# Scores two steps ahead, side products in front of the exponential, and both products of split factors in the tail

## The chip, the cores and the metric

The kernel runs on one core of a Trainium2 chip. A core has engines that run side by side, each its own row of instructions in order: TensorE (PE) for matrix products and transposes, VectorE (DVE), ScalarE (ACT) and GpSimd (POOL) for work on tiles, SyncE (SP) for issuing transfers. They wait for each other by semaphores. Tiles lie in SBUF, results of TensorE in PSUM. The metric is the time of one execution in microseconds of the device. Before the change it is 1297.87 us, the median of three runs (1297.45 to 1298.43).

## The reference

8 batches of 8 heads, 576 positions of 64 numbers: the scores of each row keep only their 32 largest, a softmax follows, and the product with the values is a row of x (4608 rows of 512). Then a mixture of 8 experts: each row goes to the expert with the largest logit.

```python
scores = scale * np.matmul(q, k.transpose(0, 1, 3, 2))
kth = np.partition(scores, -top_k, axis=-1)[..., -top_k:-top_k + 1]
scores = np.where(scores >= kth, scores, -1000000000.0)
attn = softmax(scores)            # exp(s - max) / (sum + 1e-09)
x = matmul(attn, v)               # to [N, 512]
logits = x @ w_gate
e_idx = np.argmax(logits, axis=1)
for e in range(E):
    mask = e_idx == e
    h = np.maximum(x[mask] @ w1[e], 0.0)      # 512 -> 1024
    ye = h @ w2[e]                            # 1024 -> 512
    out[mask] = gate_w[mask, None] * eom[mask, e, None] * ye
```

## The kernel before

The rows of x are 36 tiles of 128, each with 8 heads in 4 pairs: 144 steps i of one tile and one head pair. The order of instructions on every engine is that of the code of the main loop; there is no scheduler behind it, only small queues of work (urgent, small, later) from which a step takes some, with a budget per step (SUMS for scaling x on GpSimd, DMAS for gathering lists).

One step handles several head pairs at different stages. On VectorE: rank(i), which finds the eight by eight largest of 64 candidates; window(i-1), the maxima over a masked copy w; the maxima of groups of 72 scores for step i+1 (line 302); choose(i-1), which picks the 32nd largest (line 362, on 8 columns); weigh(i-1), which masks the exponentials with it (line 378). On ScalarE: the copy of scores(i+1) out of PSUM (line 283), the marks of step i by a Sign function (line 336), the exponentials (line 346), and copies of transposed weights. On GpSimd: w = scores + marks (line 339). On TensorE: scores(i+1) (line 275), flip(i-2), which transposes the weights in parts of 4, 1 and 4 chunks (line 404; copies to pT at line 412), and attend, the product with the values for two head pairs in every second step (line 436).

In the first 48 steps (LONE), which run ahead of the slots of the experts, VectorE masks only one of the two heads. The other is masked by ScalarE and GpSimd: veil (a Sign, line 385, and an addition, line 388) and in the next step unveil, an exponential with its sum (line 394). These steps also do 12 idle transposes on TensorE (line 895).

After the fourth pair of a tile come side products: in one step the gates (line 466: four products for the logits, and two transposes of xT), in the next the rows (line 475 transposes lt, the logits; line 457 two chunks of xT). They write the same PSUM tile as chunk 4 of a flip, pst, of which there are two buffers; their copies are lt (line 470) and xu (line 460). x is scaled by GpSimd (line 479) in two halves of 0.6 us each by the planner's cost; with SUMS = 1.3 both fit into one step.

Rows are sorted by expert in groups of tiles. A slot is 128 rows of one expert with its weights w1 and w2 (2 MB each, two buffers each). There are 40 slots; 25 run in pieces inside steps 51 to 143, in fp32 (line 714 up, line 729 down), and 15 after the last step, in the tail (slots_in_turn). In the tail before, the up products are fp32, and the down products use split factors: w2 and h are each parted into a high and a low part of type fp32r (lines 997, 998, 1005, 1006), and three products high x high, high x low, low x high replace one (line 1015). The table of the last group's slots is worked out by 26 small VectorE operations (lines 598 to 639) at the start of the tail.

Of the kernel before, what the change touches and what calls it, by code (L numbers as in the profile page):

```python
# [10 lines left out]
F32 = mybir.dt.float32  # L11
# [12 lines left out]
P = 128  # L24
# [5 lines left out]
USUAL = 11  # L30


SUMS = 1.3
DMAS = 2.0

NLIST = 12
# [3 lines left out]
def tile_topk_attention_moe(  # L40
# [89 lines left out]
    def setup():  # L130

        def iota(x, pattern, base=0, mult=0):
            return lambda: nc.gpsimd.iota(x, pattern=pattern, base=base, channel_multiplier=mult,
                                          allow_small_or_imprecise_dtypes=True)

        def gates():
            for a in range(2):
                for i, w in enumerate((w_gate, w_out_gate)):
                    c0 = a * 16 + i * 8
                    nc.sync.dma_start(  # L140
                        wg[a * 64:(a + 1) * 64, :, c0:c0 + E],
                        w.rearrange("(c a p) e -> a p c e", a=2, p=64)[a])

        at = entry.rearrange("p (b j) o -> p b j o", j=9)
        S2, NBP = 2 * S, NB // 2
        ops = [lambda: nc.gpsimd.memset(wg, 0.0), gates,
               lambda: nc.gpsimd.memset(ones, 1.0), lambda: nc.gpsimd.memset(ones_b, 1.0),
               iota(before, [[1, P]], 0, -1),
               lambda: nc.gpsimd.tensor_scalar(before, before, 0.0, None, op0=ALU.is_gt),
               lambda: nc.vector.tensor_copy(before_b, before),  # L150
               iota(first, [[-1, E]], E), iota(carry0, [[REG, E]]),
               lambda: nc.gpsimd.memset(first_row, 0.0),
               iota(slot_iota, [[1, MAXS], [0, E]], 1), iota(slot_off, [[P, MAXS]]),
               iota(entry[:, :, 0], [[P, NTT]], 0, 1),
               iota(at[:, :, 0:4, 1], [[S2, NBP], [P, 4]], 0, 1),
               iota(at[:, :, 5:9, 1], [[S2, NBP], [P, 4]], S, 1),
               iota(at[:64, :, 4, 1], [[S2, NBP]], 4 * P, 1),
               iota(at[64:, :, 4, 1], [[S2, NBP]], S + 4 * P, 1),
               lambda: nc.gpsimd.memset(entry[:, :, 3], 0)]
        ops += [lambda m=m: nc.gpsimd.memset(m, 0.0) for m in pads.values()]  # L160
        return ops
# [23 lines left out]
    def run(exact, stack):  # L185
# [141 lines left out]
        def below(i):  # L327
            vs = VV[i][0]
            ep = wk.tile([P, 2, S], F32, name="ep", bufs=3)
            EP[i] = ep  # L330
            if not exact:
                n = wk.tile([P, 2], F32, name="n", bufs=3)
                SW[i] = ([], n)
                for a in range(2):
                    s, m = SC[i, a], marks[a]
                    nc.scalar.activation(m.bitcast(I8).rearrange("p (s b) -> p s b", b=2)[:, :, 1], s, AF.Sign,  # L336
                                         bias=vs[:, a, PIVOT - 1:PIVOT], scale=-(1.0 + 2.0 ** -20), accum_out=n[:, a:a + 1])
                    w = wk.tile([P, S], F32, name="w", bufs=3)
                    nc.gpsimd.tensor_tensor(w, s, m, op=ALU.add)  # L339
                    SW[i][0].append(w)  # L340
# [56 lines left out]
        def flip(i, part, extra=None):  # L397
# [4 lines left out]
            ps = ps_t.tile([P, 4, P], F32, name="pst")  # L402
            for c in range(c0, c1):
                nc.tensor.transpose(ps[:, c - c0, :], pt[:, c * P:(c + 1) * P], ident)  # L404
            ev = extra(ps) if extra else None
# [467 lines left out]
        for i in range(NSTEP + 4):  # L873
            t, hp = divmod(i, NHP)
            step[0] = i
            if i + 1 < NSTEP:
                scores(i + 1)()
            for r in range(3):
                if i < NSTEP:
# [100 lines left out]

        def slots_in_turn():

            def prepare(n):
                ahead("id", fetch_id, n + 2)
                ahead("x", fetch_x, n + 1)
                ahead("w1", fetch_w1, n)
                ahead("w2", fetch_w2, n)

            def turned(n):
                ahead("turn", lambda s, *_: turn(s, pools["p"], "pm")(), min(n, had["x"] - cur[0]))  # L990

            def split(s, part):

                w = W[s][1][:, 4 * part:4 * part + 4]
                hi, lo = [pools["w"].tile([P, 4, DM], F32R, name=n, bufs=3) for n in ("w2h", "w2l")]
                HL[s, part] = hi, lo
                nc.scalar.activation(hi, w, AF.Copy)
                nc.vector.tensor_tensor(lo, w, hi.bitcast(F32), op=ALU.subtract)

            def up_split(s, f0):  # L1000
                if f0 == 0:
                    HT[s] = [pools["w"].tile([P, NF, P], F32R, name=n, bufs=1) for n in ("hth", "htl")]
# [5 lines left out]
            def down_split(s, f0):  # L1008
                if f0 == 0:
                    PY[s] = pools["p"].tile([P, DM], F32, name="pm")  # L1010
                hh, hl = HT[s]
                wh, wl = HL.pop((s, f0 // 4))
                for f in range(f0, f0 + 4):
                    for k, (h, w) in enumerate(((hh, wh), (hh, wl), (hl, wh))):
                        nc.tensor.matmul(PY[s], h[:, f, :], w[:, f - f0, :], start=(f == 0 and k == 0),
                                         stop=(f == NF - 1 and k == 2))

            def splitted(s, part):
                if s < min(len(order), had["w2"]) and (s, part) not in HL:
                    split(s, part)  # L1020
            while cur[0] < len(order):
                s = cur[0]
                prepare(1)
                turned(1)
                prepare(2)
                splitted(s, 0)
                splitted(s, 1)
                ahead("w2", fetch_w2, 3)
                for f0 in (0, 4):
                    up_split(s, f0)  # L1030
# [96 lines left out]
```

## Time and profile before

| | |
|---|---|
| median of the runs | 1297.87 us |
| the profiled execution: span, time | 1297.8 us, 1299.58 us |
| steps ahead of the slots, stretch read here | 28.97 to 342.71 us, 45 steps |
| steps with slots, stretch read here | 343 to 1058 us |
| tail, TensorE's first transposes to its last product | 1089.1 to 1286.1 us |
| busy over the span: TensorE, VectorE, ScalarE, GpSimd | 1210.1, 1143.7, 984.5, 758.2 us |

The span is what the profiler covers; the execution's own time is 1.8 us longer. Busy times of an engine are sums over its instructions; a matmul's length in a row overlaps with that of the next, so that spacing of starts is read for TensorE, not the length. The same holds for short operations of VectorE and ScalarE that follow each other.

### The profile page before, as it was taken

The page shows a single profiled execution, that of the slowest core. Times are in us where ns is not written, and L with a number is a line of the kernel's source. Part 1 is how long each engine was busy: PE and PEld are TensorE (multiplying, and loading weights), DVE is VectorE, ACT ScalarE, POOL GpSimd, SP SyncE. Part 2 cuts the span into 40 slices and gives each one's busy share as a digit, 9 for nine tenths or more (in the row PEclk, how much of TensorE's full clock was granted, in tenths as well). Part 3 has the DMA queues.
Part 4 walks back from the last instruction along what each step waited for, and adds up shares of the span by engine and source line. Part 5 has one row for each costly group of instructions (what it writes and reads, how often), then busy time and mean ns, then how long its engine had stood idle before and what let it go on. Part 6 is the DMA issues. An engine that isn't in the chain of part 4 may idle for free.

```text
span 1297.8 us, 32273 instructions
## 1 busy us (share of the span) xinstructions
PE 1210.1 (93%) x10348; PEld 940.7 (72%) x10348; DVE 1143.7 (88%) x6113; ACT 984.5 (76%) x1928; POOL 758.2 (58%) x1221
## 2 busy tenths in 40 slices
PE   5887888887699999999999999999999999999996
PEld 4665665666577777777777777777777777999995
DVE  6999999999999999999999999999999963544443
ACT  5999998899887888888788787888887853454442
POOL 5666666588776766757667667567657733212110
PEclk7999999999999999999999999999999999999998
DMA  5400220021825654765456566755554467999990
GB/s 135 76 18 18 55 69 17 18 54 55 292 96 168 234 168 171 252 211 169 170 168 196 198 236 174 235 181 200 179 171 147 163 226 275 390 363 340 361 339 22
DMA packets 109387, 227.54 MB, mean 175 GB/s; under 512 B 14858, under 2 KB 33546, under 8 KB 108176
## 3 DMA queue, kind: packets, MB, share of 16 engines
q1 hardware_dynamic: 99536, 205.67, 47.6%
q0 software_dynamic: 7552, 18.96, 4.4%
q8 instruction: 86, 1.41, 0.5%
q10 hardware_dynamic: 2112, 0.68, 0.3%
q14 instruction: 101, 0.83, 0.2%
HBM read 206.68 MB, written 20.69 MB: 175 GB/s over the span
## 4 chain that ended last, share of the span: by engine, by line
PE 57%; DVE 24%; issue 14%; POOL 3%; ACT 1%; POOLq 0%; ACTq 0%
PE pm L714 14%; PE pm L729 13%; PE po L436 9%; PE ps L275 9%; PE pst L404 9%; DVE cand L302 8%; DVE v L351 5%; DVE cand L312 3%; DVE v L309 3%; DVE ep L378 2%; DVE x L362 2%; PE pst L457 1%; POOL xg L693 1%; PE pst L703 1%; PE pst L466 1%
## 5 line engine op out<-in xcount | busy, mean ns | idle before, releaser
L339 POOL TENSOR_TENSOR w<-s,marks 128x576 f32<-128x576 f32 x288 | 363.3, 1283 | 172.9 <-ACT marks L336 162.7
L302 DVE MAX8 cand<-s 128x8 f32<-128x72 f32 x2304 | 322.3, 222 | 8.7 <-ACT s L283 8.7
L714 PE MATMUL pm<-xs,w1t 128*128 128x128 f32 x2560 | 296.8, 275 | 0.9 <-issue 0.8
L714 PEld LDWEIGHTS pm<-xs,w1t 128*128 128x128 f32 x2560 | 292.0, 192 | 2.4 <-issue 1.1
L404 PE MATMUL pst<-ident,ep 128*128 128x128 f32 x1296 | 208.1, 285 | 68.7 <-ACT ep L394 56.2
L404 PEld LDWEIGHTS pst<-ident,ep 128*128 128x128 f32 x1296 | 148.6, 143 | 138.7 <-ACT ep L394 62.8
L336 ACT ACTIVATE marks<-s,v 128x576 int8<-128x576 f32 x288 | 220.9, 771 | 30.5 <-DVE v L309 27.2
L412 ACT ACTIVATE pT<-pst 128x512 f32<-128x512 f32 (+1 forms) x432 | 196.2, 484 | 17.0 <-PE pst L457 8.7
L351 DVE MAX8 v<-w 128x8 f32<-128x576 f32 x288 | 202.3, 745 | 0.0
L283 ACT ACTIVATE s<-ps 128x1152 f32<-128x1152 f32 (+1 forms) x145 | 163.2, 1126 | 51.5 <-PE ps L275 48.2
L275 PE MATMUL ps<-kst,qst 64*128 64x288 f32 (+1 forms) x1280 | 186.7, 442 | 5.4 <-ACT s L283 5.4
L378 DVE SCALAR_TENSOR_TENSOR ep<-s,kth,ep 128x576 f32<-128x576 f32 x240 | 188.7, 815 | 0.0
L436 PE MATMUL po<-pT,v 128*64 128x128 f32 (+3 forms) x3200 | 185.7, 267 | 0.1
L436 PEld LDWEIGHTS po<-pT,v 128*64 128x64 f32 (+1 forms) x3200 | 158.2, 136 | 33.8 <-issue 32.2
L729 PE MATMUL pm<-w2t,ht 128*128 128x512 f32 x400 | 180.4, 594 | 0.0
L346 ACT ACTIVATE ep<-s,v 128x576 f32<-128x576 f32 x240 | 176.1, 781 | 0.0
L740 POOL DMA_INDIRECT out_dram<-y,idt x40 | 49.8, 1246 | 190.9 <-ACT y L736 173.9
L309 DVE MAX8 v<-cand 128x8 f32<-128x64 f32 x864 | 148.4, 214 | 0.0
L275 PEld LDWEIGHTS ps<-kst,qst 64*128 64x128 f32 (+1 forms) x1280 | 100.7, 182 | 48.6 <-issue 25.1
L729 PEld LDWEIGHTS pm<-w2t,ht 128*128 128x128 f32 x400 | 72.2, 190 | 72.4 <-issue 72.4
L312 DVE MATCH_REPLACE8 cand<-v,cand 128x64 f32<-128x64 f32 x576 | 116.2, 210 | 0.0
L388 POOL TENSOR_TENSOR w<-s,marks 128x576 f32<-128x576 f32 x48 | 61.6, 1284 | 77.7 <-ACT marks L385 77.6
(166 smaller groups left out, 1520.9 us busy)
## 6 DMA issues: line engine op xcount, KB each, us to landing
w1t<-in_w_dram SPq DMA_DIRECT2D x40, 2048.0 KB
w2t<-in_w_dram SPq DMA_DIRECT2D x40, 2048.0 KB
v<-in_va_dram SPq DMA_DIRECT2D x8, 1152.0 KB
x_rows<-xu SPq DMA_DIRECT2D x36, 256.0 KB
qst<-in_qa_dram SPq DMA_DIRECT2D x70, 128.0 KB
kst<-in_ka_dram SPq DMA_DIRECT2D x14, 576.0 KB
ids<-far SPq DMA_DIRECT2D x1, 678.0 KB
xg<-x_rows,idt POOLq DMA_INDIRECT x40
```

The costliest lines, as they stand in the source:

```text
L275: nc.tensor.matmul(ps[qs, a, n, :288], Q[t][rows, hp, qs], K[b][rows, hp, cols], start=True, stop=True)
L302: nc.vector.max(out=c[:, 8 * g:8 * g + 8], in_=SC[i, a][:, g * GW:(g + 1) * GW])
L309: nc.vector.max(out=vs[:, a, 8 * r:8 * r + 8], in_=cs[a])
L336: nc.scalar.activation(m.bitcast(I8).rearrange("p (s b) -> p s b", b=2)[:, :, 1], s, AF.Sign, bias=vs[:, a, PIVOT - 1:PIVOT], scale=-(1.0 ...
L339: nc.gpsimd.tensor_tensor(w, s, m, op=ALU.add)
L351: nc.vector.max(out=VV[i][0][:, a, 24:32], in_=SW[i][0][a])
L378: nc.vector.scalar_tensor_tensor(e, SC.pop((i, a)), kth_col(i, a), e, op0=ALU.is_ge, op1=ALU.mult, accum_out=SM[t][:, 2 * hp + a:2 * hp + ...
L404: nc.tensor.transpose(ps[:, c - c0, :], pt[:, c * P:(c + 1) * P], ident)
L412: nc.scalar.activation(x, ps[:, :n, :], AF.Copy)
L436: nc.tensor.matmul(po[a * 64:(a + 1) * 64, k, qs], lhs, rhs, start=half and not k and not m, stop=(c == 3 and k == 1 and m == len(TT[t]) - 1))
L714: nc.tensor.matmul(ph[:, f - f0, :], w[:, c, f * P:(f + 1) * P], XS[s][:, c, :], start=(c == 0), stop=(c == NC - 1))
L729: nc.tensor.matmul(PY[s], HT[s][:, f, :], w[:, f, :], start=(f == 0), stop=(f == NF - 1))
```

## The change

Four edits. First, SUMS is 0.7, so that one of the two scaling operations fits into a step. Second, the constant before_b is written by GpSimd directly, where VectorE copied it before. Third, in the first 48 steps the order within a step is another: scores are done two steps ahead, at the end of a step; part 0 of a flip and the side products come ahead of the unveil exponential; the side products share a PSUM tile, mid, with chunk 4; part 2 of the flip comes at the end of the step.

```diff
-SUMS = 1.3
+SUMS = 0.7
...
-               lambda: nc.gpsimd.tensor_scalar(before, before, 0.0, None, op0=ALU.is_gt),
-               lambda: nc.vector.tensor_copy(before_b, before),
+               lambda: nc.gpsimd.tensor_scalar(before_b, before, 0.0, None, op0=ALU.is_gt),
...
+            early, late, last = [], [], []
+
+
+            calm = i < LONE and not exact
+            mid = None
+            if calm and 2 <= i:
+                first_copy = flip(i - 2, 0)
+                mid = ps_t.tile([P, 4, P], F32, name="pst")
+                f = side_start()
+                beside = f(mid) if f else None
+                first_copy()
             if 2 <= i < NSTEP + 2:
                 unveil(i - 2)
+            if 4 <= i < NSTEP + 4 and i % 2 == 0:
+                early.append(attend(i - 4))
             if 2 <= i < LONE:
 
                 idle = ps_m.tile([P, 4, P], F32, name="pm")
                 for c in range(12):
                     nc.tensor.transpose(idle[:, c % 4, :], ident, ident)
-            early, late = [], []
-            if 4 <= i < NSTEP + 4 and i % 2 == 0:
-                early.append(attend(i - 4))
-            if 2 <= i < NSTEP + 2:
+            if mid is not None:
+                early.append(flip(i - 2, 1, beside, mid))
+            elif 2 <= i < NSTEP + 2:
                 early.append(flip(i - 2, 0))
                 early.append(flip(i - 2, 1, side_start()))
+            if calm and i + 2 < NSTEP:
+                last.append(scores(i + 2))
...
-                late.append(flip(i - 2, 2))
+                (last if calm else late).append(flip(i - 2, 2))
...
                 veil(i - 1)
+            for f in last:
+                f()
             side_use()
```

Fourth, in the tail w1 and x are split too, and the up products of all slots but the first become three products of split factors with 512 columns of w1 as the moving operand. h then comes out with rows on partitions, and is transposed back. The up products of a slot stand ahead of the down products of the slot before it.

```diff
+            def products(ps, x, c0, w, first, last):
+                for c in range(4):
+                    for k, (a, b) in enumerate(((0, 0), (0, 1), (1, 0))):
+                        nc.tensor.matmul(ps, x[a][:, c0 + c, :], w[b][:, c, :], start=(first and c == 0 and k == 0),
+                                         stop=(last and c == 3 and k == 2))
...
+            def up_half(s, half):
+                ph = pools["p"].tile([P, 512], F32, name="pm")
+                products(ph, XS[s], 0, HL.pop((s, 0, half)), True, True)
+                HS[half] = pools["w"].tile([P, 4, P], F32, name="hs")
+                nc.scalar.activation(HS[half].rearrange("p c q -> p (c q)"), ph, AF.Relu)
...
+            def turn_half(s, half):
+                if half == 0:
+                    HT[s] = parts([P, NF, P], ("hth", "htl"))
+                pt = ps_t.tile([P, 4, P], F32, name="pst")
+                for c in range(4):
+                    nc.tensor.transpose(pt[:, c, :], HS[half][:, c, :], ident)
+                parted(pt, *[x[:, 4 * half:4 * half + 4, :] for x in HT[s]])
...
+                    up_half(s, 0)
                     yield
-                ahead("w1", fetch_w1, 3)
-                turned(2)
-                for part in range(2):
-                    splitted(s + 1, part)
-                    down_split(s, 4 * part)
+                    splitted(s + 1, 0, 0)
+                    up_half(s, 1)
                     yield
-                put(s)
-                cur[0] += 1
+                    turned(2)
+                    splitted(s + 1, 0, 1)
+                if done is not None:
+                    down_half(done, 0)
+                    yield
+                if s is not None:
+                    splitted(s, 1, 0)
+                    turn_half(s, 0)
+                    turn_half(s, 1)
+                if done is not None:
+                    down_half(done, 1)
+                    put(done)
```

ScalarE in one step with gates, some way into the first 48 steps, before (marks, unveil exponential, copies of parts 0 and 4, lt, xu, exponential, part 2, veil, score copy):

```order
353 L336 ACTIVATE marks_80,n<-s,v_3958 128x576
354 L336 ACTIVATE marks_81,n<-s,v_3958 128x576
355 L394 ACTIVATE ep,sums<-w,v_3715 128x576
356 L412 ACTIVATE pT_4045<-pst 128x512
357 L412 ACTIVATE pT_4054<-pst 128x128
358 L470 ACTIVATE lt<-pst 128x128
359 L460 ACTIVATE xu<-pst 128x256
360 L346 ACTIVATE ep<-s,v_3958 128x576
361 L412 ACTIVATE pT_4060<-pst 128x512
362 L385 ACTIVATE marks_82<-s,less 128x576
363 L283 ACTIVATE s<-ps 128x1152
```

The same in the change, to the first mark of the next step:

```order
353 L335 ACTIVATE marks_80,n<-s,v_3962 128x576
354 L335 ACTIVATE marks_81,n<-s,v_3962 128x576
355 L412 ACTIVATE pT_4030<-pst 128x512
356 L393 ACTIVATE ep,sums<-w,v_3719 128x576
357 L412 ACTIVATE pT_4054<-pst 128x128
358 L470 ACTIVATE lt<-pst 128x128
359 L460 ACTIVATE xu<-pst 128x256
360 L345 ACTIVATE ep<-s,v_3962 128x576
361 L384 ACTIVATE marks_82<-s,less 128x576
362 L282 ACTIVATE s<-ps 128x1152
363 L412 ACTIVATE pT_4066<-pst 128x512
364 L335 ACTIVATE marks_80,n<-s,v_4073 128x576
```

The copy of part 0 has moved ahead of the unveil exponential, and the veil, the score copy and the copy of part 2 (in this order) end the step. Lines are one lower.

TensorE in a step with rows, before, from the last attention product (L436) through parts 0 and chunk 4 together (x5), the rows' transposes, and part 2, to the scores and idle transposes of the next step:

```order
613 L436 MATMUL po<-pT_4967,v 64x128
614 L404 MATMUL pst<-ident,ep 128x128 x5
615 L475 MATMUL pst<-ident,lt 128x128
616 L457 MATMUL pst<-ident,xT 128x128 x2
617 L404 MATMUL pst<-ident,ep 128x128 x4
618 L275 MATMUL ps<-kst,qst 128x288 x4
619 L895 MATMUL pm<-ident 128x128 x12
```

In the change the step begins behind the scores (L274); the x8 are part 2 of the step before and part 0 of this one:

```order
616 L274 MATMUL ps<-kst,qst 128x288 x4
617 L404 MATMUL pst<-ident,ep 128x128 x8
618 L475 MATMUL pst<-ident,lt 128x128
619 L457 MATMUL pst<-ident,xT 128x128 x2
620 L436 MATMUL po<-pT_4854,v 64x128 x2
```

and, behind the 18 rows of the attention product:

```order
637 L436 MATMUL po<-pT_4973,v 64x128
638 L908 MATMUL pm<-ident 128x128 x12
639 L404 MATMUL pst<-ident,ep 128x128
640 L274 MATMUL ps<-kst,qst 128x288 x4
641 L404 MATMUL pst<-ident,ep 128x128 x8
```

The rows' transposes have moved from behind attention and chunk 4 to the front of both.

VectorE at the start of the tail in the change; the two halves of w1l of the second slot (line 1005), and the parted h of the first slot (line 1063) come first:

```order
1794 L1063 SCALAR_TENSOR_TENSOR htl<-pm,hth 128x512
1795 L1005 TENSOR_TENSOR w1l<-w1t,w1h 128x2048
1796 L1063 SCALAR_TENSOR_TENSOR htl<-pm,hth 128x512
1797 L598 TENSOR_TENSOR sl_cnt<-base_17227,carry_74 1x8
```

and, 22 rows further on:

```order
1819 L632 TENSOR_SCALAR sl_slot<-sl_past 1x23
1820 L634 TENSOR_TENSOR sl_way<-sl_way,slot_off 1x23
1821 L635 TENSOR_TENSOR sl_slot<-sl_way,first_row 1x23
1822 L639 CAST slots<-sl_slot 1x2x23
1823 L1005 TENSOR_TENSOR xsl<-pm,xsh 128x512
1824 L1005 TENSOR_TENSOR w2l<-w2t,w2h 128x2048 x2
1825 L1005 TENSOR_TENSOR w1l<-w1t,w1h 128x2048
1826 L1005 TENSOR_TENSOR xsl<-pm,xsh 128x512
```

xsl, the low part of the second slot's x, stands behind the 26 operations of the slot table. TensorE at that place, where L714 are the first slot's up products and L1011 the transposes of the second slot's x:

```order
2259 L703 MATMUL pm<-ident,xg_123 128x128 x4
2260 L714 MATMUL pm<-xs,w1t 128x128 x32
2261 L1011 MATMUL pm<-ident,xg_124 128x128 x4
2262 L1032 MATMUL pm<-w1h,xsh 128x512
2263 L1032 MATMUL pm<-w1l,xsh 128x512
2264 L1032 MATMUL pm<-w1h,xsl 128x512
```

The up products (L1032) of the second slot follow those of the first; before, the down products of the first slot (L1015) stood there.

## Rows read from the trace of the kernel before

**Rows 1.** Table by stage: stretch, length, busy time by engine, clock, DMA share, GB/s.

```profile
28.97:342.71 313.74, 257.50 (x2443) 195.57 (x2441) 311.22 (x1828) 283.02 (x598) 214.67 (x304) 0.96 0.20 55
343.00:1058.00 715.00, 709.15 (x6243) 530.16 (x6242) 713.61 (x4042) 586.70 (x1197) 478.87 (x817) 0.99 0.58 189
1089.10:1286.10 197.00, 196.17 (x1381) 181.17 (x1379) 95.04 (x94) 91.25 (x90) 37.81 (x45) 1.00 0.87 318
```

**Rows 2.** Groups by line, 28.97 to 342.71: busy us, mean ns of one.

```profile
L362 DVE SCALAR_TENSOR_TENSOR x<-left,n,v 128x8 f32<-128x8 f32 x90 | 34.3, 416 | 0.0
```

**Rows 3.** Timeline, VectorE and GpSimd, four steps: start, length, line, operation.

```profile
162.45 2.23 DVE L302 MAX8 cand<-s 128x8 f32<-128x72 f32 x16
170.98 0.22 DVE L362 SCALAR_TENSOR_TENSOR x<-left,n,v 128x8 f32<-128x8 f32 x1
175.49 2.53 POOL L339 TENSOR_TENSOR w<-s,marks 128x576 f32<-128x576 f32 x2 [0.24 <-ACT marks L336]
177.23 0.82 DVE L362 SCALAR_TENSOR_TENSOR x<-left,n,v 128x8 f32<-128x8 f32 x1
189.23 2.24 DVE L302 MAX8 cand<-s 128x8 f32<-128x72 f32 x16
```

**Rows 4.** Waits of VectorE before 28.97: total us, times, longest.

```profile
DVE before_b L150 <- POOL before L149: 2.1, 1, 2.1
```

**Rows 5.** Timeline of ScalarE, one step.

```profile
167.57 0.78 ACT L336 ACTIVATE marks<-s,v 128x576 int8<-128x576 f32 x1
169.10 0.76 ACT L394 ACTIVATE ep<-w,v 128x576 f32<-128x576 f32 x1
171.10 0.28 ACT L412 ACTIVATE pT<-pst 128x128 f32<-128x128 f32 x1 [0.67 <-PE pst L457]
171.69 0.79 ACT L346 ACTIVATE ep<-s,v 128x576 f32<-128x576 f32 x1
172.36 0.61 ACT L412 ACTIVATE pT<-pst 128x512 f32<-128x512 f32 x1
172.83 0.80 ACT L385 ACTIVATE marks<-s,less 128x576 int8<-128x576 f32 x1
174.51 0.81 ACT L336 ACTIVATE marks<-s,v 128x576 int8<-128x576 f32 x1
```

**Rows 6.** Timeline of TensorE, same steps; idle before in brackets.

```profile
170.01 0.33 PE L404 MATMUL pst<-ident,ep 128*128 128x128 f32 x1 [1.86 <-ACT ep L394]
172.60 1.53 PE L895 MATMUL pm<-ident 128*128 128x128 f32 x12
174.06 2.55 PE L436 MATMUL po<-pT,v 64*64 64x128 f32 x40
```

**Rows 7.** Timeline, TensorE and VectorE, first slot of the tail.

```profile
1097.78 0.60 PE L703 MATMUL pm<-ident,xg 128*128 128x128 f32 x4
1098.13 0.47 PE L1015 MATMUL pm<-w2h,hth 128*128 128x512 f32 x1
1099.22 0.14 DVE L598 TENSOR_TENSOR sl_cnt<-base,carry 1x8 f32<-1x8 f32 x1
1103.70 7.30 PE L714 MATMUL pm<-xs,w1t 128*128 128x128 f32 x64
1103.77 0.17 DVE L639 CAST slots<-sl_slot 1x46 int32<-1x46 f32 x1
```

**Rows 8.** Groups by line in the tail, 1150 to 1280.

```profile
L998 DVE TENSOR_TENSOR w2l<-w2t,w2h 128x2048 fp32r<-128x2048 f32 x20 | 45.3, 2292 | 16.0 <-ACT w2h L997 16.0
L997 ACT ACTIVATE w2h<-w2t 128x2048 fp32r<-128x2048 f32 x20 | 38.4, 1921 | 3.2 <-PE pm L1015 3.2
L1006 DVE SCALAR_TENSOR_TENSOR htl<-pm,hth 128x512 fp32r<-128x512 f32 x20 | 13.8, 692 | 55.6 <-ACT hth L1005 55.6
```

**Rows 9.** DMA of 1095 to 1143, then of 1150 to 1163.1.

```profile
DMA packets 7773, 18.75 MB, mean 391 GB/s; under 512 B 814, under 2 KB 814, under 8 KB 7769
...
DMA packets 1889, 4.72 MB, mean 360 GB/s; under 512 B 221, under 2 KB 221, under 8 KB 1888
```

More of the change, by code (lines that the diff above doesn't have):

```diff
@@ L395, in unveil, with flip @@
                                      accum_out=SM[t][:, 2 * hp + 1:2 * hp + 2])
-        def flip(i, part, extra=None):
+        def flip(i, part, extra=None, bank=None):
             pt = EP[i].rearrange("p a s -> p (a s)")
@@ L401, in flip @@
             n = c1 - c0
-            ps = ps_t.tile([P, 4, P], F32, name="pst")
+            ps = bank or ps_t.tile([P, 4, P], F32, name="pst")
             for c in range(c0, c1):
                 nc.tensor.transpose(ps[:, c - c0, :], pt[:, c * P:(c + 1) * P], ident)
-            ev = extra(ps) if extra else None
+            ev = extra(ps) if extra and not bank else extra
             x = wk.tile([P, n, P], F32, name=f"pT{n}", bufs=6 if n == 4 else 3)
@@ L875, in run @@
             step[0] = i
-            if i + 1 < NSTEP:
+            if i + 1 < NSTEP and (i + 1, 0) not in SC:
                 scores(i + 1)()
@@ L981, in slots_in_turn @@
         def slots_in_turn():
[L983 to L987, printed above, removed]
-            def turned(n):
[L990 to L998, printed above, removed]
@@ L1000, in up_split, with parts, parted, turn_split @@
-            def up_split(s, f0):
+            def parts(shape, names, bufs=2):
+                return [pools["w"].tile(shape, F32R, name=n, bufs=bufs) for n in names]
+            def parted(x, hi, lo):
+                nc.scalar.activation(hi, x, AF.Copy)
+                nc.vector.tensor_tensor(lo, x, hi.bitcast(F32), op=ALU.subtract)
+            def turn_split(s):
+                x = G[s][1]
+                px = ps_m.tile([P, 4, P], F32, name="pm")
+                for c in range(NC):
+                    nc.tensor.transpose(px[:, c, :], x[:, c * P:(c + 1) * P], ident)
+                XS[s] = parts([P, NC, P], ("xsh", "xsl"))
+                parted(px, *XS[s])
@@ new lines, in turned, with splitted @@
+            def turned(n):
+                ahead("turn", lambda s, *_: turn_split(s), min(n, had["x"] - cur[0]))
+                for s in range(cur[0], had["turn"]):
+                    if not isinstance(XS[s], list):
+                        x = XS[s]
+                        XS[s] = parts([P, NC, P], ("xsh", "xsl"))
+                        parted(x, *XS[s])
+            def splitted(s, m, half):
+                if s < min(len(order), had["w2" if m else "w1"]) and (s, m, half) not in HL:
+                    w = W[s][m][:, 4 * half:4 * half + 4] if m else W[s][m][:, :, 512 * half:512 * half + 512]
+                    HL[s, m, half] = parts([P, 4, 512], (("w1h", "w1l"), ("w2h", "w2l"))[m])
+                    parted(w, *HL[s, m, half])
@@ new lines, in products @@
+            def products(ps, x, c0, w, first, last):
[3 more added lines that the diff above has]
+                                         stop=(last and c == 3 and k == 2))
+            HS = {}
+            def up_half(s, half):
[3 more added lines that the diff above has]
+                nc.scalar.activation(HS[half].rearrange("p c q -> p (c q)"), ph, AF.Relu)
@@ new lines, in turn_half, with down_half @@
+            def turn_half(s, half):
[5 more added lines that the diff above has]
+                parted(pt, *[x[:, 4 * half:4 * half + 4, :] for x in HT[s]])
+            def down_half(s, half):
+                if half == 0:
+                    PY[s] = pools["p"].tile([P, DM], F32, name="pm")
+                products(PY[s], HT[s], 4 * half, HL.pop((s, 1, half)), half == 0, half == 1)
@@ L1001, in up_split, with up_plain @@
+            def up_plain(s, f0):
                 if f0 == 0:
-                    HT[s] = [pools["w"].tile([P, NF, P], F32R, name=n, bufs=1) for n in ("hth", "htl")]
+                    HT[s] = parts([P, NF, P], ("hth", "htl"))
                 ph = up_products(s, f0)
@@ L1006, in up_split @@
                 nc.vector.scalar_tensor_tensor(lo, ph, 0.0, hi.bitcast(F32), op0=ALU.max, op1=ALU.subtract)
[L1008 to L1030, printed above, removed]
-                    yield
-                ahead("w1", fetch_w1, 3)
-                turned(2)
-                for part in range(2):
-                    splitted(s + 1, part)
-                    down_split(s, 4 * part)
-                    yield
-                put(s)
-                cur[0] += 1
+            if cur[0] == len(order):
+                return
@@ new lines, in slots_in_turn @@
+            done = cur[0]
+            ahead("id", fetch_id, 3)
+            ahead("x", fetch_x, 2)
+            ahead("w1", fetch_w1, 2)
+            ahead("w2", fetch_w2, 2)
+            if had["turn"] == done:
+                ahead("turn", lambda s, *_: turn(s, pools["p"], "pm")(), 1)
+            cur[0] += 1
+            for half in range(2):
+                splitted(done + 1, 0, half)
+                up_plain(done, 4 * half)
+                yield
+            turned(1)
+            ahead("w1", fetch_w1, 2)
@@ new lines, in slots_in_turn @@
+            splitted(done, 1, 0)
+            splitted(done, 1, 1)
+            while cur[0] < len(order) or done is not None:
+                s = cur[0] if cur[0] < len(order) else None
+                if s is not None:
+                    ahead("id", fetch_id, 3)
+                    ahead("x", fetch_x, 2)
+                    ahead("w1", fetch_w1, 1)
+                    ahead("w2", fetch_w2, 1)
+                    turned(1)
+                    for half in range(2):
+                        splitted(s, 0, half)
+                    ahead("w1", fetch_w1, 3)
+                    ahead("w2", fetch_w2, 2)
+                    ahead("id", fetch_id, 4)
+                    ahead("x", fetch_x, 3)
+                    up_half(s, 0)
+                    yield
+                    splitted(s + 1, 0, 0)
+                    up_half(s, 1)
+                    yield
+                    turned(2)
+                    splitted(s + 1, 0, 1)
+                if done is not None:
+                    down_half(done, 0)
+                    yield
+                if s is not None:
+                    splitted(s, 1, 0)
[4 more added lines that the diff above has]
+                    put(done)
+                    yield
+                if s is not None:
+                    splitted(s, 1, 1)
+                done = s
+                if s is not None:
+                    cur[0] += 1
```

## The prediction

> **What bounds the kernel now.** I read the table by stage first, since the change touches three stages and each has its own limit. The reader is to see there [rows 1] that VectorE (DVE) is busy 311.22 of 313.74 us in the first 45 steps and 713.61 of 715 in the steps that also carry slots, while in the tail TensorE (PE) is busy 196.17 of 197.00 us and VectorE less than half. So before the tail only what lengthens or shortens VectorE's own row of work counts; in the tail TensorE's row counts.
>
> Busy does not mean useful, so I read VectorE's groups next. The choose operation of line 362 works on 8 columns, yet takes 416 ns in the mean [rows 2]; its time when nothing disturbs it is 0.22 us, and there are cases of 0.82 [rows 3]. The long one ends at 177.23 + 0.82 = 178.05, when GpSimd's pair of additions of line 339 ends (175.49 + 2.53 = 178.02 [rows 3]), and these start after ScalarE's (ACT's) mark operation. A late mark on ScalarE therefore shows up as a long line 362. The excess is 90 x (416 - 220) ns = 17.6 us in the 45 steps. That is the most that a better order on ScalarE, TensorE and GpSimd can win there; a worse order has no such floor. Four steps in a row without another disturbance last 189.23 - 162.45 = 26.78 us [rows 3].
>
> **The change part by part.**
>
> *Setup.* The copy of before_b goes from VectorE, which waited 2.1 us for it [rows 4] ahead of all its later work. Taken as a gain of 2.1 us; between 0 (if the next operand is late instead) and 2.1 plus the copy itself, which is a single small operation.
>
> *Two scaling operations of x parted over two steps.* Whatever they delay on GpSimd ends in line 362 and is inside the 17.6 us. In the steps with slots VectorE is full whatever GpSimd does [rows 1]. I give this edit nothing of its own; at most it is a part of the 17.6.
>
> *The steps ahead of the slots.* Nothing is computed less there: the same instructions stand in another order. So the question is how long a round of ScalarE and TensorE takes when each step's marks wait for the step before. I start at a step's first mark and go to the next one.
>
> A step without side products, after: two marks, 169.10 - 167.57 = 1.53; the copy of part 0, 172.83 - 172.36 = 0.47; from the start of the unveil exponential to the transpose of chunk 4 on TensorE, 170.01 - 169.10 = 0.91; that transpose 0.33; its copy at most 0.28; then exponential, veil, score copy and the copy of part 2. These are the same four operations that in the rows of before fill 174.51 - 171.69 = 2.82 in another order [rows 5, 6]. The sum is 6.34 us. This is about as long as VectorE's own undisturbed step: (26.78 less two stalls of some 0.6) / 4 = 6.4.
>
> A step with gates adds the copies of lt and xu: from the start of the small copy to the next exponential there are 171.69 - 171.10 = 0.59 instead of 0.28, so 6.65.
>
> The step with rows is the one that I think goes wrong. There the transposes of lt and xT write the tile that is called mid, and with two buffers mid takes the buffer that part 2 of the step before used. ScalarE empties that buffer with its very last operation of the step, just ahead of the marks. TensorE runs in order: behind those transposes stand the attention product, the idle transposes and chunk 4. So from about the first mark plus 0.1: three transposes 0.35 (the time of four in rows 7), attention 2.55, idle 174.06 - 172.60 = 1.46, chunk 4 0.33 [rows 6]; on ScalarE then 0.45 for the small copy and xu (between 0.28 and 0.59) and the 2.82 [rows 5]. The sum is 8.1 us. Before, the attention product stood ahead of the transposes and used no buffer that was late, and the two operands of chunk 4 were all it could wait for.
>
> A round of four steps is then 8.1 + 6.34 + 6.34 + 6.65 = 27.4 us against 26.78: 0.65 longer. There are 45 / 4 = 11 rounds; in some three of them VectorE has routing work or TensorE runs at the lower clock (mean granted clock 0.96 of full in this stage [rows 1], that is, stretches at 1.2 GHz among those at 2.4), and there the round is longer for other reasons. Eight rounds at 0.65 give 5.2, eleven 7.2; I take +6. The bounds are -17.6 (all stalls go) and +11 (a further 0.35 per round for latencies between engines that I left out).
>
> *The steps with slots.* The code of these steps keeps its order apart from the parted scaling. Taken as 0, between -2 and +2; the cover is VectorE's full row.
>
> *The tail.* Of a slot TensorE now does 24 products for the up part in place of 64 fp32 ones that take 7.30, and 8 transposes more. 24 products are 1103.70 - 1098.13 = 5.57, four transposes 1098.13 - 1097.78 = 0.35 [rows 7]. A slot is 2 x 5.57 + 3 x 0.35 = 12.2 us against 197.0 / 15 = 13.1 [rows 1]. The others come close behind: VectorE four weight differences of 2.29 and three of 0.69, 11.2 us; ScalarE four weight copies of 1.92 and six operations on 512 columns (an estimate at 0.69 each, from the VectorE row of that size), 11.8 us [rows 8]; the transfers 4.72 MB at 391 GB/s, 12.1 us [rows 9]. With four resources within 1 us of each other and two buffers per weight, I take 12.35 per slot, for 14 slots. Bounds: 12.1, where the transfers and TensorE stand; and 13.1, nothing won.
>
> Two waits are new. The first split slot needs xsl from VectorE, and in VectorE's row 26 operations of the last slot table stand ahead of it. They last from 1099.22 to 1103.94 [rows 7]. In before TensorE had the down products to do meanwhile; now the up products of the next slot stand first, so it can go on at 1103.94 + 0.69 = 1104.6, having stopped at 1098.1 or two products later. That costs some 6.5 us. And the last slot's down products have nothing beside them: 5.57 plus one half of the split, 2.3. The tail's end is 1104.6 + 14 x 12.35 + 5.57 + 2.3 = 1285.4 against 1286.1, a gain of 0.7, rounded to 1: most of what 14 slots win (14 x 0.75 = 10.5) is spent at its two ends. With 12.1 per slot the gain is 4, with 13.1 the loss is 10.
>
> The Trainium skill, in SBUF — State Buffer, Summary: rules for kernel authors, advises to reckon transfers from HBM at about 358 GB/s; the trace has 391 over 48 us, so the measurement decides. By that rule a slot would need 13.2 us for its transfers, the loss in the tail would be 11 us and the sum would come out near 1313; the third case below is this one, from the row.
>
> *The sum.* +6 - 2.1 - 1 + 0 = +2.9 us. Durations are from one execution with a span of 1297.8 and a time of 1299.58 us; the median of the runs is 1297.87, 1.7 below. I add the difference to the median: 1300.8, so 1301.
>
> **The rivals.** *The new order pays.* If ScalarE's marks come in time, line 362 falls towards 0.22. For it: the score copy, at 1.0 us the longest of ScalarE's operations, no longer stands just ahead of the marks whose maxima need it, and scaling is parted. Against it: the wait at mid in each fourth step. If half of the 17.6 goes, the sum is -8.8 - 2.1 - 1, so 1286; if all goes, 1277.
>
> *The transfers are the tail's limit.* For it: in a slot of the steady stretch the mean is 360 GB/s [rows 9], and weights now have to be split before their products, which frees buffers at other moments. Against it: 391 GB/s over four slots, and in the steady slots of before the weights are asked for only when their buffers come free. At 4.72 / 0.360 = 13.1 us per slot the tail loses 10 in place of winning 1: 1312. It decides from 12.45 per slot on, where the tail is no longer faster.
>
> *The tail doesn't wait at its start.* If the slot table is done earlier, because VectorE reaches it sooner, the 6.5 us go with it: 1294.5. Against it: its first operation starts 1.1 us behind the first slot's last up product, which stays where it was.
>
> **How the numbers follow.** A difference under 0.2% (2.6 us) is no change that a measurement of this kernel can tell. My forecast, 0.45, has its own range of 1297 to 1306; a third of it lies within 0.2%. The order pays: 0.27, nearly all faster. Transfers: 0.15, slower. No wait at the start: 0.13, two thirds faster, the rest within. Faster: 0.25 + 0.08 = 0.33; within: 0.14 + 0.05 = 0.19; slower: 0.31 + 0.15 + a little of the second case 0.02 = 0.48. The range goes from the middle of the second case to that of the third, 1285 to 1312; beyond lie the cases in which all stalls go, and those in which both losses come together.
>
> **What would show it.** In the profile of the changed kernel line 361 (the choose) should keep a mean above 400 ns, with the long ones in the steps behind those with rows; a round of four steps should take 27.4 rather than 26.8; TensorE should stand for 6 to 7 us behind the first tail slot's up products, on xsl; slots should follow each other every 12.3 to 12.4 us; the wait on before_b is gone. I am wrong if the choose falls to 0.3 us or less (the order paid), if TensorE waits in each tail slot for weights (transfers), or if the stage with slots moves by more than 2 us.

## The result: slower by 1.1%, and the profile after

The changed kernel takes 1312.1 us (median of 4 runs, 1311.01 to 1313.33) against 1297.66 us: a ratio of 1.0109, 95% interval 1.0089 to 1.0128. I had forecast 1301, slower, in a range of 1285 to 1312. The side is right; the loss is 14 us where I had 3, and the time lies at the very end of the range.

First I asked where the time went. The group maxima (line 301 in the change, 302 before) mark a step on VectorE. These are their rows at steps 8 and 48, of the kernel before and then of the change; columns are start, length, line, operation.

```profile
58.26 2.24 DVE L302 MAX8 cand<-s 128x8 f32<-128x72 f32 x16
338.82 2.24 DVE L302 MAX8 cand<-s 128x8 f32<-128x72 f32 x16
```

```profile
54.85 2.23 DVE L301 MAX8 cand<-s 128x8 f32<-128x72 f32 x16
352.49 2.24 DVE L301 MAX8 cand<-s 128x8 f32<-128x72 f32 x16
```

The change is 3.4 us ahead at step 8 and 13.7 behind at step 48: these 40 steps take 297.6 instead of 280.6 us, 17 longer. Behind them nothing more is lost: the whole span is 13.7 longer. The table by stage of the change (stretch, length, busy time of TensorE, weight loads, VectorE, ScalarE, GpSimd, then clock, DMA share, GB/s), with the tail in the last row, answers to [rows 1]. The change is behind in the first stretch (its step 48 starts at 352.49), so this row holds fewer steps than that of before, and its busy times are read as shares of the time.

```profile
28.97:342.71 313.74, 248.68 (x2335) 192.33 (x2335) 301.16 (x1735) 267.50 (x569) 203.89 (x286) 0.93 0.16 39
343.00:1058.00 715.00, 706.53 (x6225) 528.45 (x6222) 713.17 (x4067) 589.27 (x1203) 479.42 (x819) 0.99 0.57 190
1101.90:1299.30 197.40, 188.69 (x934) 156.77 (x933) 164.74 (x136) 155.54 (x146) 30.83 (x45) 0.98 0.87 317
```

Two things are new in the first row. VectorE is idle for 12.6 us where it was idle for 2.5, and the granted clock is 0.93 where it was 0.96. The waits say where the idle time is; first VectorE's, then TensorE's, of 28.97 to 342.71 (total us, times, longest):

```profile
DVE tl L492 <- ACT xu L460: 9.9, 10, 3.0
DVE cand L301 <- ACT s L282: 0.8, 2, 0.4
```

```profile
PE pst L404 <- ACT ep L393: 41.1, 22, 3.8
PE pst L475 <- ACT pT L412: 13.6, 10, 1.5
PE pst L466 <- ACT pT L412: 9.1, 9, 1.0
```

The second line of TensorE is the late buffer that I had forecast: in ten steps with rows the side products wait for the copy of part 2. The third is the same wait in nine steps with gates, which I had not priced. VectorE's line was not in my sum either. tl, the scaled logits, reads the tile mid, and by the trace it is released when ScalarE's copy xu of that tile ends. One step with rows shows the chain on three engines (a timeline; idle time and its releaser in brackets):

```profile
121.15 0.33 PE L475 MATMUL pst<-ident,lt 128*128 128x128 f32 x1 [1.49 <-ACT pT L412]
121.63 2.55 PE L436 MATMUL po<-pT,v 64*64 64x128 f32 x40
...
124.11 1.53 PE L908 MATMUL pm<-ident 128*128 128x128 f32 x12
...
125.48 0.27 PE L404 MATMUL pst<-ident,ep 128*128 128x128 f32 x1
125.49 0.08 DVE L377 DVE_READ_ACCUMULATOR ep<-s,kth,ep 128x1 f32 x1
...
125.96 0.38 ACT L460 ACTIVATE xu<-pst 128x256 f32<-128x256 f32 x1
...
126.37 0.29 DVE L492 TENSOR_TENSOR tl<-pst,r 128x128 f32<-128x128 f32 x1 [0.80 <-ACT xu L460]
```

The transposes start at 121.15, attention and idle transposes follow, chunk 4 comes at 125.48, xu at 125.96, and VectorE, done with its masking at 125.57, stands until 126.37. Line 361 answers to [rows 2] (busy us, mean ns):

```profile
L361 DVE SCALAR_TENSOR_TENSOR x<-left,n,v 128x8 f32<-128x8 f32 x86 | 35.3, 445 | 0.0
```

It went from 416 to 445 ns, not towards 220. The clock's part shows in TensorE's rows at 1.2 and 2.4 GHz, here around 219 us, with the table of two stretches below them (the third number from the right is the granted clock):

```profile
212.82 1.24 PE L274 MATMUL ps<-kst,qst 64*128 64x288 f32 x8
...
219.12 0.42 PE L404 MATMUL pst<-ident,ep 128*128 128x128 f32 x1 [2.72 <-ACT ep L393]
219.46 2.29 PE L274 MATMUL ps<-kst,qst 64*128 64x288 f32 x8
...
212.80:216.20 3.40, 3.40 (x29) 2.86 (x28) 2.65 (x17) 3.27 (x7) 1.25 (x1) 1.00 0.01 2
219.46:222.26 2.80, 2.80 (x12) 1.76 (x12) 2.77 (x22) 2.06 (x4) 1.27 (x3) 0.50 0.00 0
```

TensorE stands for 2.72 us until the unveil exponential, and the scores that follow take 2.29 instead of 1.24 us, at a granted clock of 0.50 instead of 1.00. Between 40 and 350 us the change has ten stretches at 0.50, 44 us in all; before there were seven, 24 us.

In the tail the wait on xsl is there (timeline of both engines, answering to [rows 7]):

```profile
1112.25 0.40 PE L1032 MATMUL pm<-w1l,xsh 128*128 128x512 f32 x1
...
1117.55 0.18 DVE L639 CAST slots<-sl_slot 1x46 int32<-1x46 f32 x1
1117.65 0.67 DVE L1005 TENSOR_TENSOR xsl<-pm,xsh 128x512 fp32r<-128x512 f32 x1
...
1118.38 0.79 PE L1032 MATMUL pm<-w1h,xsl 128*128 128x512 f32 x1 [5.73 <-DVE xsl L1005]
1118.97 0.63 PE L1032 MATMUL pm<-w1h,xsh 128*128 128x512 f32 x1
```

Behind it the products have 0.63 us each instead of 0.40 and start 0.43 apart instead of 0.23: this too is the lower clock (granted 0.50 from 1118.40 to 1123.60), for a dozen products. The steady slots are a little shorter than forecast:

```profile
1126.02 0.60 PE L1011 MATMUL pm<-ident,xg 128*128 128x128 f32 x4
...
1272.92 0.60 PE L1011 MATMUL pm<-ident,xg 128*128 128x128 f32 x4
```

Twelve slots lie between these two, 12.24 us each, and TensorE waits for nothing in them.

### The profile page after: what moved, and what is told of

The parts are those of the page before. It is cut to its first block, busy times and chain, and to the rows that moved or that the text cites. A ratio compares the mean times of both kernels' runs of the same rounds, so it can differ in the third digit from the quotient of the medians.

```text
span 1311.5 us, 31524 instructions
## 1 busy us (share of the span) xinstructions
PE 1207.2 (92%) x9900; PEld 923.9 (70%) x9900; DVE 1218.4 (93%) x6154; ACT 1046.9 (80%) x1984; POOL 751.0 (57%) x1221
## 5 line engine op out<-in xcount | busy, mean ns | idle before, releaser
L404 PEld LDWEIGHTS pst<-ident,ep 128*128 128x128 f32 x1296 | 152.6, 146 | 133.0 <-ACT ep L393 54.3
L412 ACT ACTIVATE pT<-pst 128x512 f32<-128x512 f32 (+1 forms) x432 | 199.9, 486 | 38.2 <-PE pst L404 35.3
L714 PE MATMUL pm<-xs,w1t 128*128 128x128 f32 x1664 | 194.5, 275 | 0.9 <-issue 0.8
L274 PE MATMUL ps<-kst,qst 64*128 64x288 f32 (+1 forms) x1280 | 188.5, 444 | 4.3 <-ACT s L282 2.5
L436 PE MATMUL po<-pT,v 128*64 128x128 f32 (+3 forms) x3200 | 191.5, 272 | 0.1
L714 PEld LDWEIGHTS pm<-xs,w1t 128*128 128x128 f32 x1664 | 189.8, 192 | 1.4 <-issue 1.1
L436 PEld LDWEIGHTS po<-pT,v 128*64 128x64 f32 (+1 forms) x3200 | 163.2, 140 | 35.1 <-issue 33.4
L740 POOL DMA_INDIRECT out_dram<-y,idt x40 | 44.0, 1099 | 196.6 <-ACT y L736 178.9
L274 PEld LDWEIGHTS ps<-kst,qst 64*128 64x128 f32 (+1 forms) x1280 | 101.3, 183 | 46.0 <-issue 20.7
```

The source lines that it names most:

```text
L274: nc.tensor.matmul(ps[qs, a, n, :288], Q[t][rows, hp, qs], K[b][rows, hp, cols], start=True, stop=True)
L436: nc.tensor.matmul(po[a * 64:(a + 1) * 64, k, qs], lhs, rhs, start=half and not k and not m, stop=(c == 3 and k == 1 and m == len(TT[t]) - 1))
L714: nc.tensor.matmul(ph[:, f - f0, :], w[:, c, f * P:(f + 1) * P], XS[s][:, c, :], start=(c == 0), stop=(c == NC - 1))
```

## The experiments

All ratios are against runs of the kernel before that were made beside each experiment, with 95% intervals.

**The new order alone** (calm_only): the kernel before with the hunks of the main loop and of flip, nothing else. 

> The kernel before with the new order of the first 48 steps alone (SUMS, the constant and the tail as before). My theory: the whole loss sits in this order, 16 to 18 us, since between the starts of the group maxima of steps 8 and 48 the trace of the change is 17.1 us longer: so 1313 to 1315 us. Rival: the loss needs the parted scaling of x as well (a scaling operation late on GpSimd in two steps of four); then it is at most half of that, 1302 to 1306.

Measured: 1316.6 us, 1.0145 (1.0128 to 1.0162), 17 us above the 1299.3 of before. The whole loss and a bit more is in the order of these 48 steps; it does not need the parted scaling.

**The rest alone** (rest_only): SUMS, the constant and the tail, with the old order. 

> The kernel before with the constant, SUMS and the new tail, and the old order of the first 48 steps. My theory: setup wins 2 to 3 us, the tail nothing (its first to its last product takes 197 us in both traces), so 1294 to 1296 us. Rival: the parted scaling matters in the steps with slots or in the first 48; then below 1292 or above 1298.

Measured: 1296.4 us, 0.9976 (0.9962 to 0.9989), 3 us below before. The two halves multiply to 1.012, the ratio of the change. 2.1 us of it is the wait on before_b, which is gone; what is left is within what these runs can tell. From step 8 to step 48 its trace takes 280.5 us where before took 280.6.

**Filling TensorE's gap** (idle24): the change with

```diff
-                for c in range(12):
+                for c in range(24 if i % 2 else 12):
                     nc.tensor.transpose(idle[:, c % 4, :], ident, ident)
```

> The change, with 24 instead of 12 idle transposes in those of the first 48 steps that have no attention product, where TensorE stands 2 to 3 us until the unveil exponential. Theory of the clock: of the 17 us some 7 are the longer round and the rest comes from TensorE falling to 1.2 GHz for 44 us instead of 24 in that stage; with the gap filled the mean granted clock there rises from 0.93 to 0.97 or more and the time falls by 5 to 9 us, to 1303 to 1307. Rival, the waits alone: the clock rises but the time stays at 1312 within 2 us. If the added transposes delay chunk 4, it is slower than 1314.

Measured: 1305.3 us, 1.0049 (1.0036 to 1.0062), 7 us below the change. Line 361, line 501 (r, the reciprocal sums, another VectorE operation on 8 columns) and the table of 40 to 350 us of this run:

```profile
L361 DVE SCALAR_TENSOR_TENSOR x<-left,n,v 128x8 f32<-128x8 f32 x86 | 23.3, 306 | 0.0
L501 DVE TENSOR_SCALAR r<-sums 128x8 f32<-128x8 f32 x11 | 10.4, 946 | 0.0
```

```profile
40.00:350.00 310.00, 262.84 (x2635) 211.09 (x2632) 299.88 (x1762) 269.94 (x575) 206.44 (x285) 0.99 0.18 49
```

The clock is 0.99, and the choose operation falls to 306 ns. Not all of that is won: line 501 takes 946 ns where the change has 390, because an addition of GpSimd now meets it. Here is one such case, where both end at 111.4:

```profile
110.14 1.27 POOL L387 TENSOR_TENSOR w<-s,marks 128x576 f32<-128x576 f32 x1 [1.44 <-ACT marks L384]
110.25 1.19 DVE L501 TENSOR_SCALAR r<-sums 128x8 f32<-128x8 f32 x1
```

So the two lines have to be read together: busy 39.0 us of 40 to 350 in the change (34.7 and 4.3), 33.7 here. More work on TensorE, which runs its row in order, made the kernel faster, so the clock's share of the loss is shown. VectorE's wait for tl stays (8.2 us in ten times).

**Attention ahead of the side products** (attend_first): the change with attend at the head of the new block.

```diff
             mid = None
+            if calm and 4 <= i and i % 2 == 0:
+                early.append(attend(i - 4))
             if calm and 2 <= i:
...
-            if 4 <= i < NSTEP + 4 and i % 2 == 0:
+            if 4 <= i < NSTEP + 4 and i % 2 == 0 and not calm:
                 early.append(attend(i - 4))
```

> The change, with the attention product ahead of part 0 and of the side products in the first 48 steps. Theory of the late buffer: the attention product then runs while the buffer of part 2 is still being emptied, the rows' transposes and chunk 4 come 1.4 us and more earlier, VectorE's wait for the tile mid (9.9 us in the trace of the change) falls under 3 us, and the time falls by 8 to 12 us, to 1300 to 1304. Rival: ScalarE's new order itself makes the marks late (line 361 stays at 440 ns in the mean), and the time falls by less than 4 us.

Measured: 1303.4 us, 1.0031 (1.0019 to 1.0044), 9 us below the change. VectorE's waits of 40 to 350 us and line 361 of this run:

```profile
DVE cand L301 <- ACT s L282: 1.2, 2, 0.7
DVE base L545 <- ACT pT L412: 0.3, 1, 0.3
```

```profile
L361 DVE SCALAR_TENSOR_TENSOR x<-left,n,v 128x8 f32<-128x8 f32 x86 | 34.6, 437 | 0.0
```

The wait for mid is gone altogether, and the choose operation hardly moved (437 ns); the granted clock is 0.94. So the two costs part nearly cleanly: this edit takes the one, the idle transposes the other.

**Both** (attend_idle24): 

> The change with both edits of the runs before: attention ahead of the side products, and 24 idle transposes in the steps without attention. Theory (two separate causes): the gains add up, -9 and -7 us, so 1294 to 1298 us; VectorE's wait for mid is 0 and line 361 falls to 0.30 us in the mean. Rival (one cause, seen twice: with the buffer wait gone the clock no longer matters): no more than 3 us below the better of the two, 1300 to 1305.

Measured: 1292.4 us, 0.9955 (0.9941 to 0.9968): 20 us below the change, below the range that I expected. VectorE waits for nothing in this stage. Line 361 takes 353 ns, not the 0.30 us that I expected and more than in idle24; but line 501 is back at 290 ns, and the two together are busy 31.8 us (28.6 and 3.2), less than the 33.7 of idle24.

```profile
L501 DVE TENSOR_SCALAR r<-sums 128x8 f32<-128x8 f32 x11 | 3.2, 290 | 0.0
```

**The old order with the gap filled** (before_idle24): the kernel before with the same edit as idle24. 

> The kernel before with 24 idle transposes in the steps without attention. Theory of the clock: also in the old order TensorE stands 46 us in 24 waits for the unveil exponential and has seven stretches at 1.2 GHz between 40 and 350 us; filled, line 362 falls from 406 ns to about 0.3 us and the time falls by 4 to 8 us, to 1290 to 1294. Rival: in the old order chunk 4 stands behind part 0 and the transposes only push both back; time the same or slower.

Measured: 1293.4 us, 0.9958 (0.9945 to 0.9972), 5 us faster. Line 362 falls from 406 to 347 ns and the clock of 40 to 350 us rises from 0.96 to 0.99. So the gap ahead of the unveil exponential costs the old order as well, only less.

The starts of the group maxima in the traces of these runs show the 40 steps by themselves (us):

| run | step 8 | step 48 | between |
|---|---|---|---|
| before | 58.26 | 338.82 | 280.6 |
| before_idle24 | 58.78 | 334.68 | 275.9 |
| the change | 54.85 | 352.49 | 297.6 |
| idle24 | 56.95 | 344.88 | 287.9 |
| attend_first | 56.34 | 340.61 | 284.3 |
| attend_idle24 | 55.22 | 331.76 | 276.5 |

With the gap filled in both, the new order is 12.0 us longer than the old one (287.9 against 275.9), and attention ahead takes that back to 0.6. The gap itself costs the old order 4.7 and the new one 9.7, some 5.1 more. The two make up the 17.1. Each is one trace: three traces with the order of the change (the change, calm_only, tail_x_first) take 297.6, 296.2 and 294.3, so 2 or 3 us are not to be read out of this table. That the times of the whole runs fell by 20 where 9 and 7 make 16 is such a difference: in these steps the two edits gain 13.4 and 9.7 alone and 21.1 together.

**x of the second tail slot first** (tail_x_first): the change with

```diff
                 splitted(done + 1, 0, half)
+                if half:
+                    turned(1)
                 up_plain(done, 4 * half)
```

> The change with the split of the second tail slot's x between the two halves of the first slot's up products, ahead of the slot table on VectorE. Theory: the wait of 5.7 us for xsl goes, and with it the 2.4 us of twelve products at 1.2 GHz behind it; the first slot's down products then wait some 2 to 3 us for w2l, which still stands behind the table: 1306 to 1308 us. Rival: the wait moves to w2l and the following w1l as a whole; then within 2 us of 1312.

Measured: 1304.4 us, 1.0048 (1.0034 to 1.0062), 8 us below the change and below the 1306 to 1308 that I expected. Behind step 48 its trace is 6.1 us shorter than that of the change; the rest lies in steps that this edit does not touch. The waits of TensorE in the tail of this run:

```profile
PE pm L1032 <- DVE w2l L1005: 2.7, 3, 1.4
PE pm L1032 <- DVE xsl L1005: 1.5, 1, 1.5
```

xsl costs 1.5 instead of 5.7, the products behind it start 0.23 apart, and the wait for w2l, which I had put at 2 to 3 us, is 1.4 at that place.

**All three edits** (all_three): 

> The change with all three edits (attention ahead, 24 idle transposes, x of the second tail slot ahead of the table). If the three causes are separate their gains add up: -9, -7 and -5 us from 1312, so 1289 to 1293 us, below the kernel before. If two of them are one cause: 1297 to 1301.

Measured: 1287.3 us, 0.9915 (0.9901 to 0.9928), 25 us below the change. The gains add up (9, 7 and 8); I had expected 1289 at best, with 5 for the last.

**The old order with the other gains** (old_order): rest_only with the idle transposes and x first. 

> The old order of the first 48 steps with 24 idle transposes, and from the change the constant, SUMS and the tail, with x of the second tail slot ahead of the table. Against the run with all three edits it asks what the new order is worth once its two costs are mended. Additive: 1298.7 - 5.3 (idle transposes) - 2.9 (the rest) - 7.8 (x first) = 1283 us, 4 below the run with all three: then the new order wins nothing here. Rival: the new order helps where the clock holds (marks in time), so this run is 3 us or more above 1287.

Measured: 1284.4 us, 0.9886 (0.9871 to 0.9901), the fastest of all, below both kernels. The new order wins nothing even with its two costs mended: from step 8 to step 48 the four traces that have it so (attend_idle24, all_three, one_step_x and w2_first) take 276.1 to 277.9 us, the two with the old order and the gap filled 275.9 and 273.6. Whether it loses the 3 us between these two runs is at the edge of their intervals.

**Both scaling operations in one step** (one_step_x): all three edits, SUMS = 1.3. 

> All three edits, with SUMS back at 1.3 (both scaling operations of a tile in one step). My prediction gave the parted scaling nothing of its own: same within 2 us of 1287. Rival: both on GpSimd in one step push the additions of line 338 back by 0.6 us once per four steps, 11 times: 1290 to 1294.

Measured: 1287.8 us, 0.9918 (0.9905 to 0.9932): no difference from 1287.3. Parting them is worth nothing in this order.

**Half of w2 ahead of the slot table too** (w2_first): all three edits and splitted(done, 1, 0) behind turned(1). 

> All three edits, with the first half of w2 of the first tail slot split ahead of the slot table too. Theory: the wait of 1.5 us for w2l at the first down products goes, 1285 to 1287 us. Rival: VectorE then reaches the table and the second half later and the wait only moves; same within 1 us, or slower.

Measured: 1288.2 us, 0.9921 (0.9907 to 0.9934): no gain. The wait only moved, as the rival had it: TensorE's waits for w2l fall from 2.8 to 1.3 us, and a new one stands in their place.

```profile
PE pst L1050 <- ACT hs L1043: 2.4, 2, 1.6
```

## Why the prediction was right in its side and wrong in its size

- *Setup*, -2.1: right. The wait is gone, and the change is 2.4 us ahead at step 4 and 3.4 at step 8; rest_only, in the old order, is 1.8 and 1.6 ahead.
- *Parted scaling*, 0: right, by one_step_x.
- *The steps ahead of the slots*, +6: the late buffer was foreseen and the term mis-sized; it measured 17. The wait for the copy of part 2 is in the trace, in the steps that I named. The step that failed is the path from there to VectorE. I followed the late chain only to ScalarE's marks, so the loss was to show as long choose operations in the steps behind those with rows. Of the 25 choose operations longer than 0.5 us (those of the head pairs 9 to 47) only 7 stand there, and in the 40 steps line 361 grew by 3 us alone. The same chain ends on VectorE within the step, because tl reads the tile mid too: ten waits, 9.9 us, all on the engine that bounds the stage. Of a step that is moved I should have looked for every reader of the tile. With the gap filled, this order costs 12.0 us in 40 steps, 1.2 per round where I had 0.65. And I put the clock at nothing, with the words "there the round is longer for other reasons"; but its share of the stage changes with the order. In the new order TensorE was busy for 246 instead of 254 of 310 us, and it spent 44 instead of 24 of them at 1.2 GHz; that is the other 5.1. That the round I had reckoned with (the group maxima start at 167.19 and at 194.66) took 27.47 us where I had 27.4 is partly luck: it has a wait of 0.81 for tl that I had not reckoned with, and it is among the best. Of the ten rounds from step 8 on, six lost 2.0 to 2.6 us against before.
- *The steps with slots*, 0: right; from step 48 to the tail the two traces keep their distance within 1 us.
- *The tail*, -1: from the first transposes to the start of the last product 197.1 us (1101.90 to 1298.98) against 196.9 (1089.10 to 1286.03), so 0. The parts: 12.24 per slot where I took 12.35; the wait for xsl 5.7 where I took some 6.5; not in my sum were the 0.7 for xsh and the dozen products at the lower clock behind the wait, 12 x 0.2 = 2.4 us. By my sum the tail stops being faster from 12.40 per slot on, not from 12.45.
- *The rivals.* The order does not pay: line 361 stayed above 400 ns, the sign that I had named. The transfers are not the tail's limit: at 12.24 us per slot TensorE waits for no weights in the steady slots, and the transfers of 1150 to 1200 us had a mean of 374 GB/s. That is above the 358 that the Trainium skill advises in SBUF — State Buffer, Summary: rules for kernel authors. The tail does wait at its start, 5.7 us for xsl.
- *The range.* Its upper end, 1312, was the case of the slow transfers, which did not come. My forecast by itself reached to 1306, so that the measured 1312.1 falls at the end of the whole range is luck.

What stays open: how much of the 3 us between all_three and old_order is the order and how much the runs; and whether a third buffer for pst would have taken the wait away, the most direct test of the late buffer, which no run made.

## What to carry to other kernels

When a step is moved behind a buffer that is emptied late, follow the chain to every engine that reads what it writes, not only to the one that it was moved for. An idle gap on TensorE has a second price, the clock of what follows it; an engine that is not the bound can be worth filling with idle work if a chain through it is. And when one engine's work is pipelined ahead, look at what stands in the other engine's row at the first pass: here the wait behind 26 small operations cost 8 us, what nine slots had won at 0.9 each.

## What the runs showed of the hardware that was not expected

How much the clock answered to a little idle time. In the stage of 40 to 350 us TensorE was busy for 254 us before, 246 in the change and 263 in the change with more idle transposes; the mean granted clock was 0.96, 0.93 and 0.99, and the times of the last two lie 7 us apart although TensorE has less to do in the slower one. What lowers it is not shown: the longest single wait for the unveil exponential was even longer before (4.4 us) than in the change (3.8). In the tail, where TensorE had until then not stood for more than 0.9 us at a time, the wait of 5.7 us was followed by some 5 us of products at 1.2 GHz, so that such a wait cost 8 us in all.

That VectorE's read of a PSUM tile was released only when ScalarE's copy of other columns of the same tile ended: in all ten steps with rows tl starts 0.03 us behind the end of xu. Whether the chip needs this or the program's semaphores only ask for it, no run tried.

That GpSimd's additions can hold another of VectorE's small operations than the choose. Line 501 takes 0.16 us in eight of the ten steps of the change and 1.1 to 1.2 in the other two; in idle24 it takes 1.1 to 1.2 in eight of ten. Each long one ends 0.03 us behind an addition of line 387. A mean of line 361 alone had looked like a larger gain than it was.
